# Cross attention and a gated feed-forward: the head's statements in another order

## The chip, the cores and the metric

The kernel runs on one core of a Trainium2 chip. The metric is device time in microseconds of one execution. TensorE is called PE, its weight loads PEld, VectorE DVE, ScalarE ACT, GpSimd POOL, SyncE SP. Only SP, ACT and POOL issue DMAs here.

## The reference

Two stages. `x` has the shape (B, H, S, D) = (8, 8, 512, 64), `state` (8, 8, 32, 64). The first stage lets tokens read the state and the state read the tokens; the second is a gated feed-forward over all 4352 = 8 x (512 + 32) rows of width 512.

```python
scores = scale * (x @ state.T)                # per batch and head: 512 x 32
a = softmax(scores)
xread = a @ state                             # 512 x 64
a2 = softmax(scale * (state @ x.T))           # 32 x 512
sread = a2 @ x                                # 32 x 64
h = concat([xread, sread], axis=2)            # rows of 512 after heads are joined
gate = sigmoid(h @ w_gate)                    # 512 -> 1536
out = (gate * (h @ w_val)) @ w_out            # 1536 -> 512
```

## The kernel before, in words

The order of all work is written out by hand: the program runs under a manual schedule, so each engine executes its instructions in the order of the statements, and waits on semaphores for what others make. PSUM is eight banks, `G0 G1 OU S0 S1 S2 S3 AT`; a statement that writes PSUM names its bank, and waits until the bank's last reader is done.

Work is staged by batch. For batch `b`: x is loaded and cast to bf16; `xT_mm`/`xT_cp` transpose it (PE, then an eviction; from batch 2 on `at_xT_dma` lets SP's DMA do it); `S_mm` (for batch 0 in quarters, `Sq_mm`) makes scores, `S_exp` (`Sq_exp`) the exponentials `E` on ACT; `n_sum`, `n_mul` (`nq_sum`, `nq_mul`) normalise to `ab`; `aT_mm`/`aT_cp` or `aT_dma` transpose that to `aT`. `at_Eb` casts `E` to bf16 on POOL (four instructions, L200), and `rd_mm`, `rd_fin` make what the state reads.

Tokens' feed-forward uses an identity: (a @ state) @ W = a @ (state @ W). `sw_visit(b, lo, n, bank, bank, *ws)` multiplies the state with columns `lo:lo+n` of the weights (L286, L293; without `ws` it takes gate and value at once), and `sw_cp` evicts to `SW`. `sw_wide` does three such visits. `gv_mm(b, f, bank, bank)` multiplies `aT` by 128 columns of `SW` for gate and value (four products of 512 columns), `gv_th` makes tanh on ACT (L364), `gv_glu` the gated product on DVE (L369).

The product with `w_out` is one level of a seven-product scheme (Strassen-like). It needs sums of quarter matrices: of `wo` (`ht_sum(t, eng)`, T0 to T3, L400, 128x1536) and of the gated values of batch 0 (`h_sum(t, half, eng)`, L407, 128x768). `h_mm(k, c)` does the products of batch 0 (L442): 1 and 2 need `wo` itself, 5, 6, 7 and 4 need T0 to T3.

The head, lines 563 to 837, does batches 0 and 1 to the end of their `gv_mm`, the output products of batch 0, and prepares batch 2. Then `step(b, f)` loops over batches 2 to 8 and twelve column blocks.

Loads in the head: x of batch 0 on SP's queue; x of batch 1 (`load_xh`, two halves), all weights (`load_w(w, lo, n)`, L104, w = 0 for gate and 1 for value), state pieces (`load_sb`, L527), x of batch 2 and `wo` (`load_wo`, L107) on POOL's queue. A DMA issue on POOL is an instruction in POOL's row, behind its casts, products and memsets:

```python
def load_w(w, lo, n):
    src = (moe_w_gate, moe_w_val)[w].rearrange("(k p) n -> p k n", p=128)
    nc.gpsimd.dma_start((wg, wv)[w][:, :, lo:lo + n], src[:, :, lo:lo + n])
```

`zero(sTz, pool)` clears the padded state matrix (128x2048), and `pad(2, 6)` fills it from `sTc`; `sT_mm(q)`, `sT_cp(q)` transpose state pieces. `warm(n, bank)` is n matmuls on zeros. `w_keep`, `w_add` and `h_U4` combine the seven products; `w_store` writes them out.

Of the kernel before, what the change touches and what calls it, by code (L numbers as in the profile page):

```python
# [16 lines left out]
def kernel(  # L17
# [14 lines left out]
    nc = tc.nc  # L32
# [93 lines left out]
    def xT_mm(b, j, place, n=1):  # L126

        ps = held["xT", b, j] = place[0].tile((128, n, 4, 128), BF, name="xTp", tag=place[1])
        for jj in range(n):
            for k in range(4):  # L130
                h, c = 2 * (j + jj) + k // 2, k % 2 * 2
                nc.tensor.transpose(ps[:, jj, k], xhs[b][:, h, c:c + 2].rearrange("p c d -> p (c d)"), ident)

    def xT_cp(b, j, cp, n=1):
        cp(xT_tile(b)[:, j:j + n], held["xT", b, j])
# [43 lines left out]
    def Sq_exp(b, j):  # L179
        if b not in E1s:  # L180
            E1s[b] = ap_.tile((128, 4, 2, 128), FP, name="E1")
        nc.scalar.activation(quarter(b, j, E1s), held["Sq", b, j].rearrange("p c e n -> p (c e) n"), AF.Exp, scale=scale)

    def nq_sum(b, j):
        rs = ap_.tile((128, 8), FP, name="rsq", bufs=4)
        nc.vector.tensor_reduce(rs, quarter(b, j, E1s), AX.X, ALU.add)
        ri = held["riq", b, j] = ap_.tile((128, 8), FP, name="riq", bufs=4)
        nc.vector.reciprocal(ri, rs)
# [411 lines left out]
    xT_mm(1, 0, S0, 2)  # L600
    nq_sum(0, 2)
    load_w(1, 1024, 256)
    xT_cp(0, 3, act)
    load_sb(2)
    Sq_mm(0, 3, OU)
    Sq_exp(0, 1)
    nq_sum(0, 0)
    nq_sum(0, 1)
    Sq_exp(0, 3)
    nq_sum(0, 3)  # L610
    load_w(1, 0, 256)
    warm(3, G0)
    nq_mul(0, 3, vec)
    xT_cp(1, 0, act, 2)
    nq_mul(0, 0, pool)
    xT_mm(1, 2, S1, 2)
    nq_mul(0, 2, vec)
    nq_mul(0, 1, pool)
    xT_cp(1, 2, vec, 2)
    S_mm(1, 0, OU)  # L620
    S_exp(1, 0)
    load_w(1, 1280, 256)
    n_sum(1, 0)
    at_Eb(0)
    aT_mm(0, AT)
    aT_cp(0, 0, act)
    S_mm(1, 1, S2)
# [3 lines left out]
    sw_cp(0, 256, 2, 0, vec)
    S_exp(1, 1)
    n_sum(1, 1)
    rd_mm(0, AT)
    sw_cp(0, 256, 2, 1, act)
    n_mul(1, 0, pool)
    rd_fin(0)
    load_w(0, 0, 256)
    load_sb(1)
    sw_visit(1, 256, 256, OU, S3)  # L640
    sw_cp(1, 256, 2, 0, act)
    load_sb(3)
    gv_mm(0, 3, G0, S1)
    n_mul(1, 1, vec)
    gv_th(0, 3)
    load_w(0, 512, 512)
    sw_visit(0, 1024, 256, G1, AT)
    sw_cp(1, 256, 2, 1, act)
    sw_visit(1, 1024, 256, OU, G0)
    sw_cp(0, 1024, 2, 1, act)  # L650
    load_w(1, 512, 512)
    sw_cp(0, 1024, 2, 0, act)
    at_Eb(1)
    sw_cp(1, 1024, 2, 0, act)
    aT_mm(1, S0)
    gv_glu(0, 3)
    aT_cp(1, None, vec)
# [96 lines left out]
    sw_cp(1, 1280, 2, 0, act)
    h_sum(2, 0, pool)
    h_sum(2, 1, vec)
    sw_cp(1, 1280, 2, 1, act)
    gv_mm(1, 4, G1, OU)
    gv_glu(1, 6)
    cast_x(2, pool, 0, 4)  # L760
    gv_mm(1, 7, S1, AT)
    gv_th(1, 4)
    sw_cp(1, 0, 2, 1, vec)
    gv_glu(1, 4)
    gv_th(1, 7)
    gv_glu(1, 7)
    gv_mm(1, 11, S3, G1)
    h_sum(1, 1, pool)
# [7 lines left out]
    h_sum(0, 0, pool)
    h_mm(5, 0, G1)
    S_mm(2, 0, OU)
    h_mm(5, 1)
    ht_sum(2, vec)  # L780
    h_sum(1, 0, vec)
# [254 lines left out]
```

## Time and profile before

| | us |
|---|---|
| median of 3 runs | 212.94 (212.85 to 213.03) |
| the profiled execution | 213.18 |
| its span, first to last instruction | 211.4 |
| PE busy | 203.4 |
| DVE busy | 160.5 |
| ACT busy | 129.8 |
| POOL busy | 78.6 |

The span is what the trace shows of the profiled execution; the 1.8 us beside it lie before the first and after the last instruction. Busy time is the union of an engine's instructions. A row of the timeline gives start, length, engine, line, operation, output <- inputs, count, and in brackets the idle time before it with what ended it. DMA rows give size and time from issue to landing.

### The profile page before, as it was taken

To read this page: it belongs to the slowest core of one execution; us is meant where nothing else is said; L and a number is where in the kernel's file an instruction comes from. 1 tells how busy PE (TensorE), PEld (TensorE's weight loads), DVE (VectorE), ACT (ScalarE), POOL (GpSimd) and SP (SyncE) were. 2 spreads that over 40 slices of the span, in tenths; PEclk is the share of its full clock that TensorE was granted. 3 is DMA by queue.
4 is the path that set the end of the run, shared out by engine and by line. 5 is a ranking of instruction groups with operands and counts; after the bars stand their busy time and mean duration, and the time that the engine had idled before them with its cause. 6 is when DMAs were issued, how large, how long until landed. Compare 5 with 4: busy or idle time off the path is not lost.

```text
span 211.4 us, 5331 instructions
## 1 busy us (share of the span) xinstructions
PE 203.4 (96%) x2089; PEld 132.1 (62%) x2089; DVE 160.5 (76%) x308; ACT 129.8 (61%) x244; POOL 78.6 (37%) x104
## 2 busy tenths in 40 slices
PE   7679999999999999999999999999999999999993
PEld 2445443677666656565656565656566666788982
DVE  2788889998987788578876887687848876864682
ACT  4978888754767477855786578647774673233210
POOL 8899358599042705900391029301500000000010
PEclk9999999999999999999999999999999999999999
DMA  6999999671689942995923611274110500130044
GB/s 205 180 192 191 227 277 179 113 214 38 80 220 349 123 93 85 301 104 141 312 65 48 195 78 28 58 110 164 29 31 0 202 2 0 74 128 0 3 172 125
DMA packets 40921, 27.14 MB, mean 128 GB/s; under 512 B 23617, under 2 KB 38721, under 8 KB 40897
## 3 DMA queue, kind: packets, MB, share of 16 engines
q1 hardware_dynamic: 30544, 19.47, 37.1%
q0 software_dynamic: 9920, 7.01, 20.4%
q10 hardware_dynamic: 432, 0.33, 0.6%
q8 instruction: 16, 0.26, 0.6%
q14 instruction: 9, 0.07, 0.2%
HBM read 18.35 MB, written 8.91 MB: 129 GB/s over the span
## 4 chain that ended last, share of the span: by engine, by line
PE 91%; DMA 4%; POOL 2%; issue 1%; DVE 0%; POOLq 0%
PE gvp L355 30%; PE outp L425 29%; PE gvp L343 10%; PE gvp L358 5%; PE outp L442 4%; DMA wgv<-in_moe_w_val_dram 4%; PE swp L286 4%; PE outp L484 2%; PE swp L293 2%; PE Sp L147 1%; PE outp L467 1%; POOL wgv L104 1%; PE rdp L262 1%; POOL xf L100 1%; PE rdp L265 0%
## 5 line engine op out<-in xcount | busy, mean ns | idle before, releaser
L369 DVE SCALAR_TENSOR_TENSOR glu<-th,gvp 128x512 bf16<-128x512 f32 (+1 forms) x108 | 70.1, 655 | 36.6 <-PE gvp L355 13.7
L364 ACT ACTIVATE th<-gvp 128x512 f32<-128x512 f32 (+1 forms) x108 | 62.1, 578 | 49.5 <-PE gvp L355 34.8
L355 PE MATMUL gvp<-aT,SW 128*128 128x512 bf16 x288 | 77.4, 379 | 0.1
L329 ACT CAST SW<-swp 128x512 bf16<-128x512 f32 x83 | 46.7, 593 | 9.3 <-PE swp L286 8.3
L425 PEld LDWEIGHTS <-Sm 128*128 128x128 bf16 x324 | 31.7, 98 | 12.6
L355 PEld LDWEIGHTS <-SW 128*128 128x128 bf16 x288 | 26.7, 98 | 17.3 <-issue 3.1
L200 POOL CAST Eb<-E 128x256 bf16<-128x256 f32 x32 | 12.8, 438 | 52.0 <-ACT E L167 52.0
L425 PE MATMUL outp<-tw,Sm 128*128 128x256 bf16 x240 | 31.8, 273 | 0.0
L425 PEld LDWEIGHTS <-glu 128*128 128x128 bf16 x240 | 23.5, 98 | 10.2
L425 PE MATMUL outp<-wo,glu 128*128 128x256 bf16 x168 | 22.9, 273 | 0.0
L343 PE MATMUL gvp<-aT,SW 128*128 128x512 bf16 x96 | 22.6, 379 | 0.0
L509 POOL DMA_DIRECT2D out_dram<-res x1 | 0.6, 613 | 50.3 <-DVE res L433 50.3
L227 POOL TENSOR_TENSOR ab<-E,ri 128x512 bf16<-128x512 f32 x13 | 14.3, 1100 | 11.8 <-DVE ri L210 7.1
L407 DVE TENSOR_TENSOR Sm<-glu 128x768 bf16<-128x768 bf16 (+1 forms) x34 | 18.0, 536 | 0.0
L433 DVE SCALAR_TENSOR_TENSOR res<-outp,U 128x512 f32<-128x512 f32 x22 | 15.1, 686 | 1.2 <-PE outp L442 0.9
L343 PEld LDWEIGHTS <-SW 128*128 128x128 bf16 x96 | 8.7, 98 | 10.5 <-issue 1.6
L116 POOL CAST xb<-xf 128x1024 bf16<-128x1024 f32 x12 | 13.2, 1126 | 2.3 <-DMA xf<-in_x_dram 2.3
L358 PE MATMUL gvp<-xb,wgv 128*128 128x256 bf16 x96 | 12.6, 273 | 0.0
L167 ACT ACTIVATE E<-Sp 128x512 f32<-128x512 f32 x14 | 8.4, 599 | 6.9 <-PE Sp L147 5.7
L425 PE MATMUL outp<-wo,Sm 128*128 128x256 bf16 x84 | 11.5, 273 | 0.0
L358 PEld LDWEIGHTS <-wgv 128*128 128x128 bf16 x96 | 9.3, 98 | 1.3
L251 POOL CAST xs<-xf 128x1024 bf16<-128x1024 f32 x10 | 10.1, 1039 | 0.0
(106 smaller groups left out, 221.6 us busy)
## 6 DMA issues: line engine op xcount, KB each, us to landing
out_dram<-res SPq DMA_DIRECT2D x14, 512.0 KB, 3.3
xf<-in_x_dram SPq DMA_DIRECT2D x5, 1024.0 KB, 7.5
wo<-in_moe_w_out_dram POOLq DMA_DIRECT2D x3, 512.0 KB, 8.1
xf<-in_x_dram SPq DMA_DIRECT2D x4, 256.0 KB, 3.7
wgv<-in_moe_w_gate_dram POOLq DMA_DIRECT2D x4, 256.0 KB, 7.3
wgv<-in_moe_w_val_dram POOLq DMA_DIRECT2D x4, 256.0 KB, 8.7
xf<-in_x_dram POOLq DMA_DIRECT2D x1, 1024.0 KB, 10.1
xf<-in_x_dram POOLq DMA_DIRECT2D x2, 256.0 KB, 5.9
```

The costliest lines, as they stand in the source:

```text
L116: cp(xbs[b].rearrange("p c h d -> p h c d")[:, lo:lo + n], (xhs if b in xhs else xfs)[b][:, lo:lo + n])
L200: nc.gpsimd.tensor_copy(Ebs[b][:, c], E1s[b][:, c])
L227: (nc.gpsimd if eng is pool else nc.vector).tensor_tensor(half(b, i, abs_), e1, ri.unsqueeze(len(ri.shape)).to_broadcast(e1.shape), ALU.mult)
L329: cp(*sw_left.pop((b, lo, w, e)))
L343: nc.tensor.matmul(ps, SWs[b][:, g, w, fs], aTs[b][:, :, g], start=(g == 0), stop=(g == 1))
L355: nc.tensor.matmul(ps, SWs[b][:, g, w, fs], aTs[b][:, :, g], start=(g == 0), stop=(g == 1))
L358: nc.tensor.matmul(ps, (wg, wv)[w][:, j, fs], held["XS"][:, j], start=(j == 0), stop=(j == 3))
L364: nc.scalar.activation(th, held["gv", b, f][0], AF.Tanh, scale=0.5)
L369: nc.vector.scalar_tensor_tensor(glus[b][:, f], held["th", b, f], 1.0, held["gv", b, f][1], ALU.add, ALU.mult)
L407: eng.tensor_tensor(S_(b, t)[:, i], a, c, op)
L425: nc.tensor.matmul(wps[key][:, c], lhs[:, i, c * 128:(c + 1) * 128], rhs[:, i], start=(first and c == 0 and i == 0), stop=(i == NF // 2 - ...
L433: nc.vector.scalar_tensor_tensor(to, wps[key], 0.5, held["w", name], ALU.mult, ALU.add)
```

## The change

Statements of the head from line 591 to line 837 stand in another order. The instructions are the same in kind and number, but for these: some evictions and sums run on another engine (among them `xT_cp(1, 0)` from ACT to DVE, `aT_cp(1)` from DVE to ACT, `sT_cp(3)` from ACT to DVE, `ht_sum(0)` and `ht_sum(2)` from DVE to POOL, `n_mul(2, 0)`, `h_sum(2, 0)`, `h_sum(0, 0)`, `h_sum(1, 1)`, `h_sum(3, 0)` from POOL to DVE, `h_sum(2, 1)` and `h_sum(3, 1)` from DVE to POOL), and most PSUM banks are others. Two lines of the diff stand for it:

```diff
-    sw_visit(0, 256, 256, G0, G1)
+    sw_visit(0, 256, 256, S3, OU)
...
-    ht_sum(0, vec)
+    ht_sum(0, pool)
```

POOL's queue between the first weight loads and the load of x for batch 2, before. `E_177` is the exponentials of batch 0, `E_265` those of batch 1; L104 rows are weight loads, L527 state pieces, L82 is x of batch 2:

```order
L527 DMA tw<-in_state_dram 128x4x64
L104 DMA wgv<-in_moe_w_val_dram 128x4x256
L193 TENSOR_TENSOR ab<-E_177,riq 128x8x32 x2
L104 DMA wgv<-in_moe_w_val_dram 128x4x256
L200 CAST Eb<-E_177 128x256 x4
L104 DMA wgv<-in_moe_w_gate_dram 128x4x256
L227 TENSOR_TENSOR ab<-E_265,ri 128x8x64
L104 DMA wgv<-in_moe_w_gate_dram 128x4x256
L527 DMA tw<-in_state_dram 128x4x64 x2
L104 DMA wgv<-in_moe_w_gate_dram 128x4x512
L104 DMA wgv<-in_moe_w_val_dram 128x4x512
L200 CAST Eb<-E_265 128x256 x4
```

The same stretch of POOL's queue after (`E_182` is batch 0, `E_320` batch 1, L111 is `zero(sTz)`):

```order
L527 DMA tw<-in_state_dram 128x4x64
L193 TENSOR_TENSOR ab<-E_182,riq 128x8x32 x2
L200 CAST Eb<-E_182 128x256 x4
L193 TENSOR_TENSOR ab<-E_182,riq 128x8x32
L200 CAST Eb<-E_320 128x256 x4
L104 DMA wgv<-in_moe_w_val_dram 128x4x256
L227 TENSOR_TENSOR ab<-E_320,ri 128x8x64
L111 MEMSET sTz 128x2048
L104 DMA wgv<-in_moe_w_val_dram 128x4x256
L654 MEMSET xs 128x32x2
L104 DMA wgv<-in_moe_w_gate_dram 128x4x256 x2
L527 DMA tw<-in_state_dram 128x4x64 x2
```

The two value-weight loads (`load_w(1, 0, 256)` and `load_w(1, 1280, 256)`) moved behind both batches' casts, and the second of them behind `n_mul(1, 0)` and `zero(sTz)` as well; the rest of the loads follow in the same order as before, x of batch 2 and all three of `wo` directly behind the last weights.

POOL's queue toward the end of the head, before (from the load of the last third of `wo` to `n_mul` of batch 2, L227):

```order
L107 DMA wo<-in_moe_w_out_dram 128x4x512
L407 TENSOR_TENSOR Sm<-glu 128x768
L116 CAST xb<-xf 128x4x4x64
L407 TENSOR_TENSOR Sm<-Sm,glu 128x768
L407 TENSOR_TENSOR Sm<-glu 128x768
L407 TENSOR_TENSOR Sm<-glu,Sm 128x768
L227 TENSOR_TENSOR ab<-E_911,ri 128x512 x2
```

And after, from the three loads of `wo` on:

```order
L107 DMA wo<-in_moe_w_out_dram 128x4x512 x3
L116 CAST xb<-xf 128x4x4x64 x2
L407 TENSOR_TENSOR Sm<-glu 128x768
L557 COPY sTz<-sTc 64x24x32 x2
L400 TENSOR_TENSOR tw<-wo 128x1536 x2
L407 TENSOR_TENSOR Sm<-glu,Sm 128x768
L227 TENSOR_TENSOR ab<-E_852,ri 128x512
```

Two of POOL's four sums of gated values left it, two sums of `wo` (L400, twice as long in elements) came, and one of the two `n_mul` of batch 2 went to DVE.

On PE `rd_mm(0)` and `rd_mm(1)` stand earlier (`rd_mm(1)` before the first `gv_mm`, where it stood behind twelve of them), `sT_mm(3)` later, `warm(3)` some 2 us of work earlier. The products of batch 0 begin with `h_mm(2, 0)`, after twenty `gv_mm` instead of twenty-two.

More of the change, by code (lines that the diff above doesn't have):

```diff
@@ L601 @@
     nq_sum(0, 2)
[L602 to L605, printed above, removed]
+    xT_cp(1, 0, vec, 2)
+    Sq_mm(0, 3, G1)
     Sq_exp(0, 1)
-    nq_sum(0, 0)
+    xT_mm(1, 2, G0, 2)
+    nq_mul(0, 0, pool)
     nq_sum(0, 1)
+    xT_cp(1, 2, vec, 2)
     Sq_exp(0, 3)
+    S_mm(1, 0, S0)
     nq_sum(0, 3)
-    load_w(1, 0, 256)
[L612 to L618, printed above, removed]
@@ L619 @@
-    xT_cp(1, 2, vec, 2)
-    S_mm(1, 0, OU)
-    S_exp(1, 0)
-    load_w(1, 1280, 256)
[L623 to L627, printed above, removed]
-    load_w(0, 1280, 256)
-    aT_cp(0, 1, act)
-    sw_visit(0, 256, 256, G0, G1)
[L631 to L637, printed above, removed]
+    nq_mul(0, 2, pool)
+    S_mm(1, 1, OU)
+    at_Eb(0)
+    nq_mul(0, 1, vec)
+    rd_mm(0, S2)
@@ new lines @@
+    nq_mul(0, 3, pool)
+    nc.scalar.activation(pre[:, 0:1], ones, AF.Exp)
+    S_exp(1, 0)
+    aT_mm(0, AT)
+    S_exp(1, 1)
+    at_Eb(1)
+    rd_fin(0)
+    n_sum(1, 0)
+    load_w(1, 0, 256)
+    sw_visit(0, 256, 256, S3, OU)
+    aT_cp(0, 0, act)
+    n_mul(1, 0, pool)
+    sw_visit(1, 256, 256, G1, S1)
+    zero(sTz, pool)
+    aT_cp(0, 1, act)
+    sw_cp(0, 256, 2, 1, act)
+    rd_mm(1, S0)
+    sw_cp(0, 256, 2, 0, vec)
+    n_sum(1, 1)
+    gv_mm(0, 2, S3, S2)
+    sw_cp(1, 256, 2, 1, act)
@@ new lines @@
+    n_mul(1, 1, vec)
+    gv_th(0, 2)
+    load_w(1, 1280, 256)
+    sw_cp(1, 256, 2, 0, act)
+    sw_visit(1, 1024, 256, AT, OU)
+    rd_fin(1)
+    sw_visit(0, 1024, 256, G0, S1)
+    sT_mm(2, S3)
+    aT_mm(1, G1)
+    sw_cp(0, 1024, 2, 0, vec)
+    sT_cp(2, vec)
+    nc.gpsimd.memset(xs[:, :, :, D:], 1.0)
+    sw_cp(1, 1024, 2, 1, act)
+    sw_cp(0, 1024, 2, 1, act)
+    sw_cp(1, 1024, 2, 0, vec)
+    gv_mm(0, 3, S0, OU)
+    aT_cp(1, None, act)
+    load_w(0, 1280, 256)
+    gv_mm(0, 9, G0, S1)
@@ L642 @@
+    sT_mm(1, AT)
+    sw_cp(0, 0, 2, 1, act)
     load_sb(3)
-    gv_mm(0, 3, G0, S1)
-    n_mul(1, 1, vec)
-    gv_th(0, 3)
+    gv_glu(1, 3)
+    sw_cp(0, 0, 2, 0, vec)
+    gv_mm(1, 9, OU, G1)
     load_w(0, 512, 512)
[L647 to L650, printed above, removed]
-    load_w(1, 512, 512)
[L652 to L657, printed above, removed]
@@ L764 @@
-    gv_glu(1, 4)
[L765 to L768, printed above, removed]
+    sT_cp(1, act)
+    gv_mm(0, 1, G0, S2)
+    gv_th(1, 9)
+    gv_glu(0, 8)
+    gv_mm(0, 0, S3, S0)
+    load_w(1, 512, 512)
+    gv_glu(1, 9)
+    gv_th(0, 1)
+    sw_visit(0, 512, 512, G1, OU, 0)
+    gv_th(0, 0)
+    gv_glu(0, 1)
+    sw_cp(0, 512, 0, 1, vec)
+    sw_cp(0, 512, 0, 0, act)
+    gv_glu(0, 0)
+    gv_mm(0, 10, S1, AT)
+    gv_mm(0, 11, G0, S3)
+    gv_th(0, 10)
+    gv_th(0, 11)
@@ new lines @@
+    sT_cp(3, vec)
+    gv_glu(1, 5)
+    gv_mm(1, 6, G1, OU)
+    gv_th(1, 6)
+    sw_visit(1, 1280, 256, AT, G0)
+    h_sum(0, 0, vec)
+    h_sum(2, 1, pool)
+    sw_cp(1, 0, 2, 1, act)
+    sw_cp(1, 1280, 2, 1, act)
+    h_sum(2, 0, vec)
+    at_xT_dma(2)
+    sw_cp(1, 1280, 2, 0, act)
+    gv_mm(1, 7, S3, S1)
+    gv_mm(1, 4, G1, G0)
+    h_sum(1, 0, vec)
+    pad(2, 6)
+    S_mm(2, 0, S2)
+    h_sum(3, 0, vec)
+    ht_sum(0, pool)
+    gv_th(1, 7)
+    h_mm(2, 0, AT)
+    gv_th(1, 4)
+    gv_glu(1, 6)
@@ new lines @@
+    sw_cp(1, 0, 2, 0, act)
+    S_exp(2, 0)
+    ht_sum(2, pool)
+    h_mm(2, 1)
+    gv_glu(1, 7)
+    h_mm(1, 0, S3)
+    S_mm(2, 1, S0)
+    h_mm(1, 1)
+    gv_glu(1, 4)
+    n_sum(2, 0)
+    h_sum(1, 1, vec)
+    gv_mm(1, 10, G0, S1)
+    ht_sum(1, vec)
+    h_mm(5, 0, G1)
+    h_sum(3, 1, pool)
+    gv_th(1, 10)
+    w_keep('V1', 1)
+    S_exp(2, 1)
+    h_mm(5, 1)
+    gv_mm(1, 1, G0, OU)
+    load_x(3, nc.sync)
+    n_mul(2, 0, vec)
+    h_mm(6, 0)
+    h_mm(6, 1)
+    w_add(2, 'V1', w_res(0, 0)[:, :, lo_])
@@ L769 @@
+    gv_th(1, 1)
+    gv_glu(1, 1)
+    w_keep('U2', 1)
+    gv_mm(1, 0, AT, S2)
+    n_sum(2, 1)
+    n_mul(2, 1, pool)
+    gv_th(1, 0)
+    gv_glu(1, 10)
+    gv_mm(1, 11, G0, S3)
+    aT_dma(2, 0)
     gv_th(1, 11)
-    at_xT_dma(2)
-    gv_mm(1, 10, G0, S1)
+    gv_glu(1, 0)
+    cast_x(3, pool, 4, 4)
     gv_glu(1, 11)
-    h_mm(1, 0, AT)
-    h_mm(1, 1)
-    ht_sum(0, vec)
[L776 to L781, printed above, removed]
```

234 lines of the change are left out of this document (82 added, 152 removed).

## Prediction

> **What bounds the kernel now.** I read the page's span and busy times first, then the busy time by stretches, to see where TensorE (PE) is idle at all.
>
> ```profile
> span 211.4 us, 5331 instructions
> PE 203.4 (96%) x2089; PEld 132.1 (62%) x2089; DVE 160.5 (76%) x308; ACT 129.8 (61%) x244; POOL 78.6 (37%) x104
> ```
>
> ```profile
> 0.00:16.00 16.00, 11.83 (x167) 6.13 (x167) 9.78 (x28) 11.12 (x20) 14.80 (x27) 1.00 1.16 192
> 16.00:53.00 37.00, 36.98 (x442) 20.64 (x434) 33.29 (x56) 26.97 (x53) 27.59 (x31) 1.00 0.94 176
> ```
>
> Columns: stretch, length, then busy time of PE, PEld, DVE, ACT and POOL, granted clock, DMA share, GB/s. PE idles 4.2 us before 16 us and 0.02 us from there to the end of the head at 53. So the most that any order of the head can win is a part of 4.2 us, and whatever makes PE wait after 16 us is paid in full, for no gap is left to absorb it. POOL is the engine to look at beside it, with 14.80 of the first 16 us busy. DMA moves 192 GB/s there, so each 256 KB block takes 1.3 us of the stream.
>
> The stream is fed by POOL. Its rows, in order of time, show where the weight loads (L104) stand among its other work:
>
> ```profile
> 8.01 0.77 POOL L104 DMA_DIRECT2D wgv<-in_moe_w_val_dram  x1
> 9.35 1.19 POOL L193 TENSOR_TENSOR ab<-E,riq 128x256 bf16<-128x256 f32 x2 [0.57 <-DVE riq L188]
> 10.48 0.81 POOL L104 DMA_DIRECT2D wgv<-in_moe_w_val_dram  x1
> 11.28 1.42 POOL L200 CAST Eb<-E 128x256 bf16<-128x256 f32 x4
> ...
> 17.40 0.79 POOL L104 DMA_DIRECT2D wgv<-in_moe_w_val_dram  x1
> 18.13 1.47 POOL L200 CAST Eb<-E 128x256 bf16<-128x256 f32 x4
> 19.50 1.84 POOL L111 MEMSET sTz<- 128x2048 bf16 x1
> 21.25 0.93 POOL L82 DMA_DIRECT2D xf<-in_x_dram  x1
> ```
>
> The DMA view gives issue to landing. Its rows below are those of the first x load on POOL's queue (issued at 2.73), `load_w(1, 0, 256)` (8.01), `load_w(1, 1280, 256)` (10.48), `load_w(1, 512, 512)` (17.40), `load_wo(2)` (32.34), and, for comparison, four x loads on SP's queue:
>
> ```profile
> xf<-in_x_dram POOLq DMA_DIRECT2D x1, 256.0 KB, 5.3
> wgv<-in_moe_w_val_dram POOLq DMA_DIRECT2D x1, 256.0 KB, 9.3
> wgv<-in_moe_w_val_dram POOLq DMA_DIRECT2D x1, 256.0 KB, 8.4
> wgv<-in_moe_w_val_dram POOLq DMA_DIRECT2D x1, 512.0 KB, 11.0
> wo<-in_moe_w_out_dram POOLq DMA_DIRECT2D x1, 512.0 KB, 6.4
> xf<-in_x_dram SPq DMA_DIRECT2D x4, 256.0 KB, 3.7
> ```
>
> Issue plus landing time: the five POOL loads land at 8.0, 17.3, 18.9, 28.4 and 38.7 us. A wait of 8 to 11 us for 256 or 512 KB, where the same bytes need 1.3 or 2.6 us, is queueing: POOL issues far ahead, and the stream is never empty. What PE waits for at the end of that stream stands in its weight-load rows:
>
> ```profile
> 28.46 0.14 PEld L286 LDWEIGHTS <-tw 64*32 64x32 bf16 x16 [0.31 <-DMA wgv<-in_moe_w_val_dram]
> ```
>
> At 28.46 PE starts the first product with `wgv[512:1024]` of the value weights, 0.05 us after they landed. This gate has no slack: delay the stream by d and PE is late by d.
>
> **The change part by part.** *Loads on POOL.* In the new order `load_w(1, 0, 256)` stands behind `at_Eb(1)`, and `load_w(1, 1280, 256)` behind `n_mul(1, 0, pool)` and `zero(sTz, pool)`. When is `at_Eb(1)` free to run? It casts the exponentials of batch 1, and these hang on the second half of its x:
>
> ```profile
> 10.19 0.62 PE L132 MATMUL xTp<-ident,xf 128*128 128x128 bf16 x8 [0.43 <-DMA xf<-in_x_dram]
> 10.64 0.40 PE L156 MATMUL Sp<-tw,xT 128*128 128x64 bf16 x8
> 11.08 0.60 ACT L167 ACTIVATE E<-Sp 128x512 f32<-128x512 f32 x1 [0.64 <-PE Sp L156]
> 11.27 0.68 DVE L135 COPY xT<-xTp 128x1024 bf16<-128x1024 bf16 x1
> ```
>
> Transposes from 10.19 (unchanged: they wait for a DMA), eviction, scores, exponential: 10.2 + 0.62 + 0.68 + 0.40 + 0.60, some 12.6 with the hand-offs. POOL has `nq_mul(0, 3, pool)` ahead (0.6, half of the 1.19 row), whose sum DVE makes only after that eviction, at 11.5; it ends at about the same time, so 12.7 is a fair start. Then 1.4 for the four casts: `load_w(1, 0, 256)` is issued at 14.1, not 8.0. Its issue takes 0.77, `n_mul` 1.10 (POOL's row for L227, below) and `zero` 1.84: `load_w(1, 1280, 256)` at 17.8, not 10.5, when the load before it, landing near 18.7, is all that the stream still holds. So it starts on a nearly empty stream. How long it then takes no row shows. The nearest are 5.3 (the first load, beside SP's four), 5.1 (6.4 for 512 KB, less 1.3 for the second half, at a time when the stream had run low) and, from below, SP's 3.7. I take 4.6, between them, since nothing runs beside it; the ends are 3.7 and 5.3. It lands at 22.4 instead of 18.9: the stream is 3.5 us late (2.6 to 4.2).
>
> Behind it everything is issued in time (POOL has no other work until all of it is out, some 26 us), in the order of before, so landings keep their distance: `load_w(1, 512, 512)` 28.4 - 18.9 = 9.5 behind, at 31.9; `load_wo(2)` 19.8 behind, at 42.2.
>
> The Trainium skill ("DMA: Bandwidth & Descriptors", section "Anatomy of one DMA — SWDGE (gpsimd) path") gives about 2.0 us fixed plus bytes at 436 GB/s; by that page 256 KB would land in an estimated 2.6 us and the sum below would be some 2 us smaller. The 5.3 and 5.1 of this trace speak against it.
>
> *PE at the gate.* Until the gate PE does the same twelve `gv_mm` as before. `rd_mm(1)` moves ahead of it, `sT_mm(3)` and one `sw_visit` behind it. Costs from the chain of waits:
>
> ```profile
> 28.46 0.63 PE swp L286 x16
> 29.09 0.35 PE rdp L265 x32
> 29.43 0.28 PE rdp L268 x8
> ...
> 44.12 0.23 PE Sp L147 x8
> 44.35 0.86 PE gvp L343 x4
> 45.22 0.66 PE outp L442 x6
> ```
>
> A `gv_mm` is 0.86, a visit 0.3, `rd_mm` 0.63, `S_mm` (and `sT_mm`, also eight small products) 0.23, an `h_mm` 0.66. Net work behind the gate: 0.63 - 0.3 - 0.23, 0.1 less. PE is late by 31.9 - 28.46 - 0.1 = **3.3 us**. What PE saves before 16 us (`rd_mm(0)` and `rd_mm(1)` now fill the wait for the first weights) is worth nothing, since it waits longer at the gate; the same cover pays for the moved `warm(3)` and for `xT_cp(1, 0)` on DVE and `aT_cp(1)` on ACT. If the stream were not late, the gate at 28.4 would still hold, and the saving would be that 0.1.
>
> *wo and the first h_mm.* After the gate stand 3 visits, 8 `gv_mm`, `sw_wide` (as 3 visits), 2 visits, `sT_mm` and `S_mm`: 0.9 + 6.9 + 0.9 + 0.6 + 0.5 = 9.8 (a visit's own row counts 0.1 of drain, which I take off once), so `h_mm(2, 0)` comes at 41.6. Its last two products need `load_wo(2)`, 0.44 later at 42.0 against 42.2: **0.2**. In the old order ten `gv_mm` stood here.
>
> *T sums on POOL.* `ht_sum(0)` and `ht_sum(2)` go from DVE to POOL, twice the length of POOL's other sums:
>
> ```profile
> L400 DVE TENSOR_TENSOR tw<-wo x2: 951/952/954, 40.0 to 40.8; 128x1536 bf16<-128x1536 bf16 x2
> L407 POOL TENSOR_TENSOR Sm<-glu 128x768 bf16<-128x768 bf16 x2 | 3.3, 1640 | 0.3 <-DVE glu L369 0.3
> L407 POOL TENSOR_TENSOR Sm<-glu,Sm 128x768 bf16<-128x768 bf16 x1 | 2.3, 2291 | 2.4 <-DVE Sm L407 2.4
> L227 POOL TENSOR_TENSOR ab<-E,ri 128x512 bf16<-128x512 f32 x13 | 14.3, 1100 | 11.8 <-DVE ri L210 7.1 <-DVE rr L273 4.5
> L116 POOL CAST xb<-xf 128x1024 bf16<-128x1024 f32 x12 | 13.2, 1126 | 2.3 <-DMA xf<-in_x_dram 2.3
> ```
>
> Twice 1.64 to 2.29 is 3.3 to 4.6 where DVE took 0.95. Started at 42.2 when wo is there, T0 is ready at 45.5 to 46.8. `h_mm(5, 0)` needs it, after the rest of `h_mm(2, 0)` (0.22), three `h_mm`, `S_mm` and a `gv_mm`: 42.2 + 3.3 = 45.5. A wait of 0 to 1.3; I take **0.4**, nearer the 1.64 that two of three such sums took. The Trainium skill ("GPSIMD Engine Reference", section "4.1 Engine selection") calls POOL about twice as slow as DVE for such sums; by that estimate T0 takes 1.9 and this term is nothing. The rows here say more than three times.
>
> *What else hangs on POOL and SP.* Batch 2 goes through both twice: x lands, POOL casts it, SP transposes it for `S_mm`; later POOL finishes `ab`, SP transposes that for the steady loop. SP's transposes, and the first product of the loop:
>
> ```profile
> xf<-in_x_dram POOLq DMA_DIRECT2D x1, 1024.0 KB, 10.1
> xT<-xb SPq DMA_TRANSPOSE x24, 2.5
> 35.99 5.21 SPq L140 DMA_TRANSPOSE xT<-xb  x4
> 53.57 0.61 PE L355 MATMUL gvp<-aT,SW 128*128 128x512 bf16 x2
> ```
>
> x was issued at 21.25, landed at 31.35, and now lands 3.5 later at 34.9. Two casts of 1.13, then transposes issued 1.3 apart, each landing in 2.5: the second, which `S_mm(2, 0)` needs, at 41.0 (PE comes at 41.4), the fourth, for `S_mm(2, 1)`, at 43.6 (PE: 43.7). Just hidden, 0 to 0.5. Then T2 (3.3), `h_sum(3, 1)` (1.64), `n_mul(2, 1)` (1.10) and two transposes (1.3 + 2.5) follow T0: 45.5 + 9.8 = 55.3, up to 4 us more with the slower sums, against 53.57 + 3.9 = 57.5 for the loop's first product. Hidden, 0 to 1.5. `n_mul(2, 0)` on DVE leaves POOL 1.1 for less than that there. Other evictions and sums change engine, but DVE (33.29 of 37 us) and ACT (26.97) keep gaps: 0, up to 0.3 if a bank is late.
>
> *Sum.* 3.3 + 0.2 + 0.4 = 3.9 us. The profiled execution took 213.18 (span 211.4), 0.24 above the median of 212.94; it would become 217.1, the median **216.8**.
>
> **The rivals.**
>
> *The empty stream answers fast.* If a load on an empty queue lands like the smallest store,
>
> ```profile
> out_dram<-res SPq DMA_DIRECT2D x1, 64.0 KB, 1.8
> ```
>
> plus 1.3 for its bytes, in 3.1, then `load_w(1, 1280, 256)` lands at 20.9, the gate opens at 30.4 (PE 1.8 late), and with 0.2 + 0.4 the time is 215.3. For it: nothing runs beside the load. Against it: 5.3 and 5.1 on this very queue. The skill's page named above, with its 2.6, would end near 214.8.
>
> *POOL's tail decides.* All its sums at 2.29 a half: T0 costs 1.3 and the steady loop waits 0.9 for `aT`: 3.3 + 0.2 + 1.3 + 0.9 = 5.7, 218.6. For it: the 2.29 row, taken while DVE summed too, as it will again. Against: two of three rows at 1.64.
>
> *Late, but not felt.* The weights are late by less than PE's new lead. The lead is 0.1, and a time within 0.2% (0.43 us, about what a measurement of this kernel can tell from no change) leaves room for 0.5 in all. But issued at 17.8 and with 1.3 us of bytes the load can't land before 19.1, 0.2 later than before, so this takes a load that starts at once, or a POOL that is through by 14. It would end at 213.0.
>
> *Faster: the stream catches up.* After its pauses every queue is drained, and the 9.5 us from `load_w(1, 1280, 256)` to the gate could shrink. Below 28.4 - 22.4 = 6.0 us the gate opens earlier than before, and PE, with `rd_mm` done early, gains: at 5.2, 0.8 us, 212.1. Against it: those 9.5 us hold two blocks of 256 KB, two of 64 and two of 512, 1.66 MB, which at the stream's 192 GB/s take 8.7.
>
> **How the numbers follow.** Forecast 0.60, fast empty stream 0.17, POOL's tail 0.15, not felt 0.05, faster 0.03. So slower 0.92, same 0.05, faster 0.03. The range runs from 214.8, a little under the fast stream's case, to 218.8, just over the POOL tail's; it covers 3.7 to 5.3 for the landing (215.9 to 217.5 with the rest as summed).
>
> **What would show it.** In the changed kernel: L104 issues near 14.1 and 17.8; a dip in GB/s near 15 and 19; landing times of 4 to 5 us for `load_w(1, 1280, 256)`; PE idle of some 4 us between 21 and 32, released by DMA of `wgv`, longest before `sw_visit(0, 1280, 256)` and the 512-wide visits; 3.3 us or more a T sum on POOL. Wrong would be: PE idle 0 there, POOL getting to `load_w(1, 0, 256)` before 11 us, or a granted clock under 1.00 in the new gaps.

## The result and the profile after

The changed kernel takes 222.7 us (median of 4 runs, 221.95 to 223.07), the kernel before beside it 212.99 (212.85 to 213.55): a ratio of 1.044 [1.040, 1.047], 9.7 us slower. The forecast was 3.9 us slower, its range ended at 218.8. The profiled execution took 223.06 us.

Span, PE's busy row and the same kind of stretches as before, now of the changed kernel (its head ends near 63):

```profile
span 221.3 us, 5326 instructions
PE 207.1 (94%) x2089; PEld 133.3 (60%) x2089; DVE 166.7 (75%) x309; ACT 129.3 (58%) x243; POOL 81.6 (37%) x104
```

```profile
0.00:16.00 16.00, 12.54 (x183) 7.12 (x184) 8.49 (x25) 8.83 (x18) 13.22 (x27) 0.93 1.04 177
16.00:63.00 47.00, 39.79 (x412) 21.02 (x419) 40.56 (x59) 28.90 (x55) 31.65 (x31) 0.99 0.88 148
```

PE idles 3.5 us before 16 us (4.2 before the change) and 7.2 us behind it, where it had idled 0.02. Its busy time grew as well, by 3.7 us, in part because the clock was low near 14 to 17 us. What it waits for, in the table of waits (us in total, times, longest):

```profile
PE Sp L147 <- DMA xT<-xb: 2.7, 2, 2.5
PE swp L293 <- DMA wgv<-in_moe_w_gate_dram: 2.0, 1, 2.0
PE gvp L343 <- DVE res L433: 1.2, 1, 1.2
...
PE outp L442 <- DVE tw L400: 0.6, 1, 0.6
...
PE swp L286 <- DMA wgv<-in_moe_w_val_dram: 0.4, 1, 0.4
PE outp L442 <- DVE res L433: 0.4, 1, 0.4
```

The forecast spoke of the two `wgv` lines. The scores of batch 2 waiting for transposed x (`xT`), and the three lines released by DVE, it had at 0 to 0.8 us together; they are 4.9.

First the part that was foreseen. POOL's timeline gives the issues of the two value-weight loads, and the DMA view their time to landing and that of `load_w(1, 512, 512)`:

```profile
14.74 0.81 POOL L104 DMA_DIRECT2D wgv<-in_moe_w_val_dram  x1
15.57 1.06 POOL L227 TENSOR_TENSOR ab<-E,ri 128x512 bf16<-128x512 f32 x1
16.56 1.81 POOL L111 MEMSET sTz<- 128x2048 bf16 x1
18.31 0.81 POOL L104 DMA_DIRECT2D wgv<-in_moe_w_val_dram  x1
...
22.85 0.78 POOL L104 DMA_DIRECT2D wgv<-in_moe_w_val_dram  x1
```

```profile
wgv<-in_moe_w_val_dram POOLq DMA_DIRECT2D x1, 256.0 KB, 4.0
wgv<-in_moe_w_val_dram POOLq DMA_DIRECT2D x1, 512.0 KB, 9.6
```

18.31 + 4.0 puts `load_w(1, 1280, 256)` at 22.3, 3.4 later than before; 22.85 + 9.6 puts the last value weights at 32.45. PE's timeline shows the gate and the places behind it:

```profile
25.19 0.41 PE L293 MATMUL swp<-wgv,tw 64*32 64x512 bf16 x8 [1.95 <-DMA wgv<-in_moe_w_gate_dram]
...
32.48 0.84 PE L286 MATMUL swp<-wgv,tw 64*32 64x512 bf16 x24 [0.39 <-DMA wgv<-in_moe_w_val_dram]
...
44.93 0.29 PE L147 MATMUL Sp<-sTz,xT 128*128 128x64 bf16 x4 [2.52 <-DMA xT<-xb]
...
52.22 1.48 PE L442 MATMUL outp<-tw,Sm 128*128 128x256 bf16 x12 [0.62 <-DVE tw L400]
54.86 1.46 PE L343 MATMUL gvp<-aT,SW 128*128 128x512 bf16 x6 [1.16 <-DVE res L433]
...
63.71 1.04 PE L355 MATMUL gvp<-aT,SW 128*128 128x512 bf16 x4
```

The gate opens at 32.48 instead of 28.46, and the steady loop's first product comes at 63.71 instead of 53.57. So of 10.1 us, 4.0 arise up to the gate and 6.1 behind it, and these 6.1 the forecast had at 0.6.

Where they arise is seen on DVE and POOL side by side, DVE first:

```profile
48.31 3.85 DVE L400 TENSOR_TENSOR tw<-wo,tw 128x1536 bf16<-128x1536 bf16 x1
52.09 2.12 DVE L227 TENSOR_TENSOR ab<-E,ri 128x512 bf16<-128x512 f32 x1
54.13 0.68 DVE L433 SCALAR_TENSOR_TENSOR res<-outp,V 128x512 f32<-128x512 f32 x1
```

```profile
44.88 6.47 POOL L400 TENSOR_TENSOR tw<-wo 128x1536 bf16<-128x1536 bf16 x2 [2.48 <-DMA wo<-in_moe_w_out_dram]
51.31 2.35 POOL L407 TENSOR_TENSOR Sm<-glu,Sm 128x768 bf16<-128x768 bf16 x1
```

DVE's T1 took 3.85 us where such a sum took 0.95 before. It starts while POOL does T2 (the second of POOL's two T sums) and ends at 52.16, 0.8 after POOL's end at 51.35, about its own length. `n_mul(2, 0)` starts beside POOL's `h_sum(3, 1)` and ends 0.55 after that one's end. The `w_add` behind them (L433) at 54.13 frees the bank for which `gv_mm(1, 0)` waits.

The readings to test: **A**, the late weight loads; **B**, the transposes of batch 2 go slowly because the `w_out` loads still stream beside them; **C**, a two-input sum on DVE stands still while POOL does one. The rival to all is the granted clock, which fell to 0.50 near 14 to 17 us.

### The profile page after: what moved, and what is told of

The parts are those of the page before. It is cut to its first block, busy times and chain, and to the rows that moved or that the text cites. A ratio compares the mean times of both kernels' runs of the same rounds, so it can differ in the third digit from the quotient of the medians.

```text
span 221.3 us, 5326 instructions
## 1 busy us (share of the span) xinstructions
PE 207.1 (94%) x2089; PEld 133.3 (60%) x2089; DVE 166.7 (75%) x309; ACT 129.3 (58%) x243; POOL 81.6 (37%) x104
## 4 chain that ended last, share of the span: by engine, by line
PE 71%; DMA 11%; POOL 6%; DVE 6%; issue 3%; SPq 1%; ACT 0%; DVEq 0%; POOLq 0%; ACTq 0%
PE gvp L355 29%; PE outp L425 28%; DMA xf<-in_x_dram 9%; PE gvp L358 5%; DMA xT<-xb 3%; PE swp L286 3%; PE outp L484 2%; POOL wgv L104 2%; DVE tw L400 2%; PE outp L467 1%; PE Sp L147 1%; DVE glu L369 1%; PE swp L293 1%; DVE ab L227 1%; POOL xb L116 1%
## 5 line engine op out<-in xcount | busy, mean ns | idle before, releaser
L200 POOL CAST Eb<-E 128x256 bf16<-128x256 f32 x32 | 13.5, 454 | 51.7 <-ACT E L167 51.7
L407 DVE TENSOR_TENSOR Sm<-glu 128x768 bf16<-128x768 bf16 (+1 forms) x35 | 20.0, 576 | 0.0
L227 POOL TENSOR_TENSOR ab<-E,ri 128x512 bf16<-128x512 f32 x12 | 12.6, 1050 | 14.2 <-DVE ri L210 9.5
L433 DVE SCALAR_TENSOR_TENSOR res<-outp,U 128x512 f32<-128x512 f32 x22 | 15.0, 683 | 0.7 <-PE outp L442 0.4
L329 DVE CAST SW<-swp 128x512 bf16<-128x512 f32 x13 | 8.8, 686 | 4.4 <-PE swp L293 3.3
L407 DVE TENSOR_TENSOR Sm<-Sm,glu 128x768 bf16<-128x768 bf16 (+1 forms) x18 | 10.0, 555 | 0.2
```

The lines of the kernel that those rows point to most:

```text
L200: nc.gpsimd.tensor_copy(Ebs[b][:, c], E1s[b][:, c])
L227: (nc.gpsimd if eng is pool else nc.vector).tensor_tensor(half(b, i, abs_), e1, ri.unsqueeze(len(ri.shape)).to_broadcast(e1.shape), ALU.mult)
L329: cp(*sw_left.pop((b, lo, w, e)))
L407: eng.tensor_tensor(S_(b, t)[:, i], a, c, op)
L433: nc.vector.scalar_tensor_tensor(to, wps[key], 0.5, held["w", name], ALU.mult, ALU.add)
```

## The experiments

### The loads alone, in the order of before

The kernel before, with POOL's order of casts, loads and fills from the change: `load_w(1, 0, 256)` behind `at_Eb(1)`, the later loads behind `n_mul(1, 0)` and `zero`.

```diff
     n_sum(1, 1)
+    at_Eb(1)
+    load_w(1, 0, 256)
+    n_mul(1, 0, pool)
+    zero(sTz, pool)
+    load_w(1, 1280, 256)
+    load_w(0, 1280, 256)
...
```

> The kernel before, with one thing of the change alone: the order of the weight loads on POOL's queue (at_Eb(1) ahead of load_w(1,0,256), then n_mul(1,0) and zero, then the other loads). Theory A (the late weight stream costs PE 4.0 us at the gate before the product sums, and nothing else of the change belongs to it): load_w(1,0,256) is issued near 14.5 us instead of 8.0, the w_val tile of 512 columns lands about 32 instead of 28.4, and the kernel takes 216.0 to 217.2 us. If the loads also push the x2 and w_out loads behind them into the transposes of batch 2, 218.5 to 219.5. Rival (the loads are late but not felt; the loss comes from the sums and the transposes): 212.8 to 213.5.

Measured: 219.4 us (218.45 to 221.26), ratio 1.028 [1.026, 1.031]. That is more than theory A's 216.0 to 217.2. The number lies in the expectation's second range, but by luck: PE waits for no transposes here. In this order the first late tile that PE needs is `load_w(0, 0, 256)`, which lands behind `load_w(0, 1280, 256)`, the first that the changed kernel needs; so the pause is longer, and the clock falls behind it. PE's timeline, and the clock by stretches (the third column from the right):

```profile
27.60 1.06 PE L293 MATMUL swp<-wgv,tw 64*32 64x512 bf16 x16 [4.24 <-DMA wgv<-in_moe_w_gate_dram]
28.59 3.59 PE L343 MATMUL gvp<-aT,SW 128*128 128x512 bf16 x8
```

```profile
27.00:33.00 6.00, 5.40 (x41) 2.41 (x42) 2.69 (x5) 2.62 (x5) 0.00 (x0) 0.50 1.26 231
```

Eight products take 3.59 us; the same eight take 1.90 at full clock, in the next run. The four runs of this kernel had mean clocks of 0.981 (221.26 us), 0.980 (219.59), 0.992 (219.21) and 0.999 (218.45). So even the run with hardly any loss of clock is 5.5 us above the kernel before: that is the lateness.

### The same, with PE kept busy in the pause

```diff
+    warm(18, AT)
     sw_visit(0, 0, 256, AT, S2)
```

> The kernel before with the late weight loads (219.4 us), and 18 matmuls without use on PE in the 4.2 us in which it waits for the first late tile. If the half-speed clock of 26.7 to 33.7 us (7 us at 0.50, some 3 us of work lost) comes from that pause of PE, the granted clock stays at 1.00 and the time falls to 216 to 217.3 us, with the wait for the tile itself unchanged. If the clock falls for another reason, or its loss is hidden by the gate, the time stays at 218.5 to 220.

Measured: 218.65 us (218.12 to 219.32), ratio 1.026 [1.022, 1.029]. The clock by stretches, in the same place:

```profile
27.00:33.00 6.00, 5.94 (x62) 2.69 (x60) 4.68 (x8) 4.64 (x10) 1.27 (x2) 1.00 1.20 238
```

With PE busy in the pause there is no half-speed stretch in the profiled execution, so the pause is its likely cause. But it seems that a pause doesn't always bring it: one of the four runs above, without the extra matmuls, had a mean clock of 0.999 (its trace is not at hand). The median fell by only 0.75 us, not 2 to 3, and the two sets of runs overlap: what is left is the lateness itself. The profiled execution of this kernel starts the steady loop at 58.51, 4.9 after 53.57. I had carried 4.0 us over from the changed kernel, and this order has 4.9 of it.

### The changed kernel with early loads

```diff
...
     load_sb(2)
+    load_w(1, 0, 256)
+    load_w(1, 1280, 256)
...
     n_sum(1, 0)
+    load_w(0, 1280, 256)
+    load_w(0, 0, 256)
+    n_mul(1, 0, pool)
+    load_w(0, 512, 512)
...
```

> The changed kernel, with the weight loads of value row 1 issued early again, right behind load_sb(2), and the other weight loads behind n_sum(1,0). Theory A: the gate comes back to within 0.7 us of 28.5, 4 us are won there; if the transposes of batch 2 and the slowed sums cost what they cost in the changed kernel, 218 to 219 us. If the early stream also takes the w_out loads away from the transposes, 215.5 to 216.5. Rival (the loads are not the cause): 222 to 223.

Measured: 222.87 us (222.29 to 223.5), ratio 1.046 [1.044, 1.049]: nothing won, as the rival had it. But the gate did come earlier, at 30.10, and the wait for `xT` fell to 0.74. The time went elsewhere: PE, DVE and POOL of this run, in that order:

```profile
48.97 1.87 PE L343 MATMUL gvp<-aT,SW 128*128 128x512 bf16 x4 [4.73 <-DVE glu L369]
```

```profile
40.33 3.44 DVE L407 TENSOR_TENSOR Sm<-Sm,glu 128x768 bf16<-128x768 bf16 x1
43.80 3.32 DVE L407 TENSOR_TENSOR Sm<-glu,Sm 128x768 bf16<-128x768 bf16 x1
47.05 1.87 DVE L369 SCALAR_TENSOR_TENSOR glu<-th,gvp 128x512 bf16<-128x512 f32 x3
```

```profile
40.08 6.63 POOL L400 TENSOR_TENSOR tw<-wo 128x1536 bf16<-128x1536 bf16 x2
```

With `wo` there earlier, POOL starts its two T sums at 40.08, and now they meet two `h_sum` of DVE, each 3.3 to 3.4 us: each lasts about as long as one T sum. Such a sum in the kernel before:

```profile
41.72 0.55 DVE L407 TENSOR_TENSOR Sm<-Sm,glu 128x768 bf16<-128x768 bf16 x1
```

The `gv_glu` behind the two start at 47.05, and PE stands still for 4.73 us, followed by 0.50 clock near 49 to 52. Late weights had kept these sums apart.

### The changed kernel with its two T sums on DVE

```diff
-    ht_sum(0, pool)
...
-    ht_sum(2, pool)
...
+    ht_sum(0, vec)
     n_sum(2, 0)
...
     ht_sum(1, vec)
+    ht_sum(2, vec)
```

> The changed kernel, with the two T sums that it gave to POOL (ht_sum(0) and ht_sum(2)) back on DVE. Theory C (VectorE and GpSimd slow each other while both run sums of two inputs): ht_sum(1) takes 1.0 us on DVE instead of 3.85, the waits ahead of h_mm(6,0), gv_mm(1,0) and h_mm(4,0), 2.1 us together, are gone, and the kernel takes 220.3 to 221.0 us. Rival (those waits end with other work that is just as late, the clock or the transposes): 222.2 to 222.8.

Measured: 220.18 us (219.63 to 222.47), ratio 1.036 [1.030, 1.041]. Theory C's 220.3 to 221.0, a little better. `ht_sum(1)` is back at its length, and the T sum that meets POOL's remaining `h_sum(3, 1)` (50.14 to 52.35) is stretched instead. Its DVE rows:

```profile
49.91 0.95 DVE L400 TENSOR_TENSOR tw<-wo,tw 128x1536 bf16<-128x1536 bf16 x1
50.77 2.39 DVE L400 TENSOR_TENSOR tw<-wo 128x1536 bf16<-128x1536 bf16 x1
```

### Both together

The early loads (here with the two state loads ahead of the 512-column ones) and the T sums on DVE.

```diff
...
     n_sum(1, 0)
+    load_w(0, 1280, 256)
+    load_w(0, 0, 256)
+    load_sb(1)
+    load_sb(3)
+    n_mul(1, 0, pool)
...
+    ht_sum(0, vec)
...
+    ht_sum(2, vec)
...
```

> The changed kernel with both edits: the weight loads early (the two state loads now ahead of the 512-column tiles) and the two T sums of POOL on DVE. Apart they moved the time by +0.2 and -2.5 us. If each edit hides the other's loss (with early loads the first two T sums on POOL start near 40 us, beside DVE's sums of the products, and hold those up), the two together win much more than their sum: the wait of 4.7 us ahead of gv_mm(1,10) and the half-speed clock behind it go, and the kernel takes 214.8 to 216.5 us. If the effects simply add: 220.2 to 220.6. The product-sum gate is expected near 29.5 us (30.1 with the early loads alone, 32.5 in the changed kernel).

Measured: 218.31 us (217.75 to 219.68), ratio 1.025 [1.020, 1.030]. The prices don't add (medians, us):

| | T sums on POOL | T sums on DVE |
|---|---|---|
| loads late | 222.7 | 220.2 |
| loads early | 222.9 | 218.3 |

Early loads win 1.9 us once POOL no longer holds DVE up, and nothing while it does. That the time stayed above the expected 214.8 to 216.5 has two places, seen in its waits, which the next runs take up:

```profile
PE gvp L343 <- DVE res L433: 2.0, 1, 2.0
PE aTp L234 <- POOL ab L227: 1.4, 1, 1.4
```

### No w_out loads beside the transposes

The changed kernel without its second and third `w_out` load (1.0 MB), which sets two thirds of `w_out` to zero on DVE at the start.

```diff
+    nc.vector.memset(wo[:, 4:12], 0.0)
...
-    load_wo(1)
-    load_wo(2)
```

> The changed kernel without its second and third w_out load: two thirds of w_out are set to zero, so the last product leaves out two thirds of its weights. It takes 1.3 MB or so out of the stream between the x2 load and the transposes of batch 2. Theory B (the transposes are slow because the w_out loads still stream beside them): the transposes land 2.5 to 3.5 us after issue instead of 7.4, the wait of 2.5 us ahead of the scores of batch 2 is gone, and the kernel takes 219.7 to 220.5 us. Rival (the transposes are slow for a reason of their own): 222.2 to 222.9 with the wait in its place.

Measured: 225.2 us (224.4 to 225.5), ratio 1.057 [1.054, 1.059]: slower, where B expected a gain. On its own point B is right. The transposes in the DMA view, first of the changed kernel, then of this run:

```profile
xT<-xb SPq DMA_TRANSPOSE x4, 5.7
```

```profile
xT<-xb SPq DMA_TRANSPOSE x4, 2.5
```

The wait ahead of the scores of batch 2 fell from 2.52 to 0.05 us. But POOL's T sums started earlier (43.51), met DVE's `h_sum`, and PE's only long wait behind 40 us is

```profile
PE gvp L343 <- DVE glu L369: 5.7, 1, 5.7
```

the same place as with early loads. Part of the extra time lies at the start, where PE waited 2.5 us for x of batch 1 (0.7 in the changed kernel) and the clock was 0.51 from 14 to 21 us; the gate opens at 33.53, 1.0 later. Why that load was late isn't shown.

### One more POOL instruction, that reads or that only writes

The kernel before, with work on POOL that nobody needs, in a region of `tw` that is free then.

```diff
     h_sum(0, 0, pool)
+    pr = tw[:, -1024:]
+    nc.gpsimd.tensor_tensor(pr, pr, pr, ALU.subtract)
```

> The kernel before with one more instruction on POOL, that nobody needs: a two-input subtraction of 1024 bf16 columns (some 2.2 us) behind h_sum(0,0), at 40.0 us, while DVE does its T sums. Theory C, that a two-input sum on DVE and a POOL instruction that reads SBUF exclude each other for the whole instruction: one of DVE's T sums, 0.95 us alone, takes 2.5 to 3.2 us, the product that needs it (h_mm(5,0) at 41.1 or h_mm(7,0) at 42.6) is late by about as much less its slack, and the kernel takes 214.2 to 215.3 us. If the two engines only slow each other by their share of a port: DVE's sums 1.0 to 1.9 us, 213.2 to 214.0. If there is nothing between them: 212.9 to 213.1.

Measured: 214.56 us (214.34 to 214.72), ratio 1.0068 [1.0048, 1.0088]: +1.6 us, theory C. POOL, DVE and PE rows:

```profile
39.71 1.89 POOL L778 TENSOR_TENSOR tw<-tw 128x1024 bf16<-128x1024 bf16 x1
```

```profile
39.76 3.52 DVE L400 TENSOR_TENSOR tw<-wo 128x1536 bf16<-128x1536 bf16 x2
```

```profile
42.46 0.82 PE L442 MATMUL outp<-tw,Sm 128*128 128x256 bf16 x6 [1.42 <-DVE tw L400]
```

POOL took 1.89 us, not the 2.2 expected. DVE starts 0.05 us behind it; its two T sums take 3.52 us and end at 43.28. POOL's end (41.60) plus the 1.82 that the two take alone would be 43.42. So it is not a shared rate: the first sum gets next to nothing until POOL is done. The control has two fills in that place.

```diff
     h_sum(0, 0, pool)
+    pr = tw[:, -1024:]
+    nc.gpsimd.memset(pr, 0.0)
+    nc.gpsimd.memset(pr, 0.0)
```

> The control of the run with the extra POOL subtraction: at the same place two POOL fills of the same 1024 columns (some 1.9 us together), which write SBUF and read nothing. The Trainium skill, page "SBUF — State Buffer", section "Who interferes with whom", says that a DVE instruction with two SBUF inputs contends with a GpSimd instruction that reads SBUF, and not with one that only writes it. By an exclusion of readers alone the kernel takes 212.9 to 213.2 us and DVE's T sums keep 0.95 us. If any POOL instruction holds DVE's sums up: 214.0 to 215.0, with T sums of 2 to 3 us.

Measured: 212.95 us (212.87 to 213.42), ratio 0.9992 [0.9977, 1.0008]: no change. Again POOL, then DVE:

```profile
39.62 0.95 POOL L778 MEMSET tw<- 128x1024 bf16 x1
40.62 0.95 POOL L779 MEMSET tw<- 128x1024 bf16 x1
```

```profile
39.69 1.82 DVE L400 TENSOR_TENSOR tw<-wo 128x1536 bf16<-128x1536 bf16 x2
```

The same 1.9 us of POOL beside the same two sums, and they take 1.82. The two runs agree with what the control's expectation takes from the Trainium skill ("SBUF — State Buffer", section "Who interferes with whom").

### The T sums alone, in the kernel before

```diff
-    ht_sum(0, vec)
+    ht_sum(0, pool)
...
-    ht_sum(2, vec)
+    ht_sum(2, pool)
```

> The kernel before with one part of the change alone: its first and third T sum (ht_sum(0), ht_sum(2)) on POOL in place of DVE, at the same place in the order. POOL does them at 38.4 to 41.6 us and, behind h_sum(0,0), at 43.2 to 46.4. By the prediction's price (POOL's time, and DVE untouched) h_mm(5,0) waits 0.4 us and the kernel takes 213.0 to 213.8 us. By the exclusion of DVE's two-input sums while POOL reads SBUF, h_sum(1,0) and ht_sum(1) on DVE end only after POOL's sums, ht_sum(1) near 47 instead of 43.1, h_mm(6,0) at 43.3 waits for it, and the kernel takes 215.5 to 218 us.

Measured: 218.06 us (216.99 to 219.1), ratio 1.023 [1.017, 1.029]. The number is about the upper end of what was expected of the exclusion (215.5 to 218), but by luck: the way there is another. POOL, then PE:

```profile
39.76 3.09 POOL L400 TENSOR_TENSOR tw<-wo 128x1536 bf16<-128x1536 bf16 x1 [1.64 <-PE gvp L343]
42.81 1.63 POOL L407 TENSOR_TENSOR Sm<-glu 128x768 bf16<-128x768 bf16 x1
44.40 3.08 POOL L400 TENSOR_TENSOR tw<-wo 128x1536 bf16<-128x1536 bf16 x1
```

```profile
44.49 1.46 PE L442 MATMUL outp<-tw,Sm 128*128 128x256 bf16 x6 [3.46 <-POOL Sm L407]
```

`h_mm(5, 0)` also needs `h_sum(0, 0)`, and that stands behind T0 in POOL's queue: ready at 44.44. So the long sum first costs by its place in the queue (3.46 us), and then by the clock, which is 0.50 from 45 to 50 us in the profiled execution. DVE's stretched `h_sum(1, 0)` (3.42 us) lies behind that. The run at clock 1.000 still took 216.99 us.

### What is left

`n_mul(1, 0)` ahead of the six later loads in the run with both edits:

```diff
     n_sum(1, 0)
+    n_mul(1, 0, pool)
     load_w(0, 1280, 256)
...
-    n_mul(1, 0, pool)
```

> The run with early loads and the T sums on DVE (218.3 us), with n_mul(1,0) on POOL ahead of the six later weight loads in place of behind four of them: there PE waited 1.4 us for it ahead of aT_mm(1). If that wait is passed on to the end, 216.8 to 217.3 us; if PE stalls for other things by as much, 218.0 to 218.5.

Measured: 217.29 us (216.85 to 218.28), ratio 1.020 [1.016, 1.024]. PE's wait of 1.4 us for `n_mul` is gone, and the gate opens at 28.98, 0.5 after that of before. The longest wait that is left behind the gate, 1.6 us for DVE, is the same collision once more: DVE's T2 starts at 45.15 beside POOL's `h_sum(3, 1)` (44.52 to 46.73) and takes 2.40 us.

And with every product sum on the engine of before:

```diff
...
-    h_sum(2, 1, pool)
+    h_sum(2, 1, vec)
...
-    n_mul(2, 0, vec)
+    n_mul(2, 0, pool)
...
```

> The run with the loads behind n_mul(1,0), with the engine of every product sum as in the kernel before as well (four h_sums and n_mul(2,0) to POOL, two h_sums to DVE); the order of the statements and the PSUM banks stay those of the changed kernel. If the rest of the loss lies in DVE's load of sums (gv_mm(1,0) waits 2.0 us for a bank that DVE frees late), the kernel takes 214.3 to 215.3 us, and order and banks alone cost about 2 us. If they cost nothing, 212.8 to 213.5. If POOL's sums hold DVE's up again, 217 to 219.

Measured: 216.22 us (215.83 to 217.58), ratio 1.017 [1.011, 1.022]: above the 214.3 to 215.3 expected, though the wait for DVE ahead of `gv_mm(1, 0)` is gone. Order and banks, with the evictions that stayed on their new engines, keep some 3.2 us. Some 1.2 us of it are more small waits (4.1 us in its table of waits against 2.9 before, without the 1.0 at the start; 0.8 of them for `xT`); the rest stays open.

From PE's timelines, the gate, the loop's first product, and what lies between (one profiled execution each):

| kernel | gate | loop | between |
|---|---|---|---|
| before | 28.46 | 53.57 | 25.1 |
| changed | 32.48 | 63.71 | 31.2 |
| changed, loads early | 30.10 | 62.93 | 32.8 |
| changed, T sums on DVE | 34.61 | 63.30 | 28.7 |
| both, `n_mul` ahead | 28.98 | 57.69 | 28.7 |
| and sums as before | 29.16 | 56.16 | 27.0 |

With early loads, from the third row down, the T sums cost 4.1 us (with the half clock behind the wait of 4.73), the engines of the other sums 1.7, order and banks 1.9. For the changed kernel itself such differences are no clean prices: in the fourth row the clock fell ahead of the gate in the profiled execution, the gate came later, and PE waited 1.0 us for `xT` instead of 2.7. There the waits are the better account of the 6.1 us: 2.7 for `xT`, 2.2 for DVE's late sums and evictions, and 1.2 that has no wait of its own (PE is busy 26.37 us between gate and loop, where it was 25.11); what that is stays open. None of these versions beats the kernel before.

## Why the prediction was wrong

The sign was right, and the mechanism that it forecast is there; but it makes 4.0 of the 10.1 us up to the steady loop. The other 6.1 lie in terms that it had at nearly nothing: 0.2 for `wo`, 0 to 0.5 for the transposes, 0.4 for the T sums, 0 to 0.3 for the other sums on DVE.

*Loads on POOL: right.* Issues forecast at 14.1 and 17.8, measured 14.74 and 18.31. Landing forecast 4.6 us after issue, measured 4.0. The estimate of 2.6 that the prediction worked out from the Trainium skill ("DMA: Bandwidth & Descriptors", section "Anatomy of one DMA — SWDGE (gpsimd) path") and set aside was too low here. The stream was 3.4 us late, forecast 3.5; that this is so close is luck, for an issue 0.5 later and a landing 0.6 faster cancel.

*PE at the gate: right, 4.0 for 3.3.* The landings did not quite keep their distance: 10.1 us from `load_w(1, 1280, 256)` to the last value weights, not 9.5. That the clock would fall was named as a sign of error. It fell to 0.50 near 14 to 17 us, but ahead of a gate set by DMA, where it costs little: the run of the changed kernel at clock 1.000 took 221.95 us, the others 222.35 to 223.07. At full clock it is still 9.0 us slower than before, so the clock is not the cause of the loss.

*wo and the first h_mm, 0.2, and the transposes, "Just hidden, 0 to 0.5": wrong by 2.5 us.* `load_wo(2)` was forecast to land at 42.2. Its rows have 26.73 for the issue and 17.8 to landing, 44.5; the transposes start at 37.44. First these, then the first transpose before the change:

```profile
26.73 0.74 POOL L107 DMA_DIRECT2D wo<-in_moe_w_out_dram  x1 [0.65 <-DMA wgv<-in_moe_w_gate_dram]
37.44 6.29 SPq L140 DMA_TRANSPOSE xT<-xb  x4
wo<-in_moe_w_out_dram POOLq DMA_DIRECT2D x1, 512.0 KB, 17.8
xT<-xb SPq DMA_TRANSPOSE x2, 7.0
```

```profile
xT<-xb SPq DMA_TRANSPOSE x1, 3.5
```

The first step that failed is this one: it priced the transposes at 2.5 us, the median of all 24, and didn't see that `wo` would now still stream when they start. Before, `wo` had landed at 38.7, and even so the first transpose, issued at 35.99, took 3.5 us. In the changed kernel the pair needed for `S_mm(2, 0)` landed 7.0 us after issue, and without two `wo` loads the four took 2.5. Faster transposes alone would not have won all of the wait: PE was ready for `S_mm(2, 0)` at 42.41, so by the prediction's own count `h_mm(2, 0)` would have needed the last `wo` at 43.1 and waited some 1.4 us for it (an estimate from these rows).

*T sums on POOL, 0.4: the right duration and the wrong victim.* This is the second step that failed. T0 and T2 took 6.47 us together, just under the forecast 3.3 each. `h_mm(5, 0)` didn't wait for them; PE had already been held. The price was paid on DVE, by "Other evictions and sums change engine, but DVE (33.29 of 37 us) and ACT (26.97) keep gaps: 0, up to 0.3 if a bank is late" and by "`n_mul(2, 0)` on DVE leaves POOL 1.1 for less than that there". `n_mul` took 2.12 us on DVE, and PE waited 2.2 us for DVE's late sums and evictions. That step looked for room in DVE's busy time and took each sum's length as its own; what decides is which POOL instruction runs at that moment. Undoing the two T sums won 2.5 us with late loads and 4.6 with early ones (there with the state loads moved too).

The sign of it stood in the prediction's own rows. Of the three `h_sum` on POOL that it shows, one took 2.29 us against 1.64 (a fourth, which it doesn't count, took 1.89). I called that "while DVE summed too" and let it lengthen POOL's sums in a rival; that DVE can be the one to stand, for as long as the POOL sum lasts, I did not ask. The Trainium skill ("SBUF — State Buffer", section "Who interferes with whom") says so: a DVE instruction with two SBUF inputs and a GpSimd instruction that reads SBUF share a port, the one that comes first has it to its end, and the other waits wholly. The added POOL reader and the added POOL fills agree with it on both sides.

*The rivals.* "POOL's tail decides" (218.6) was nearest, with a longer chain behind T0, though its mechanism, a late `aT`, isn't the one that was seen. The fast empty stream, with its 3.1 to landing, is refuted by the 4.0; "not felt" and "the stream catches up" by the gate at 32.48.

## What to carry to other kernels

Before a sum moves between VectorE and GpSimd, lay the two engines' timelines side by side. Count a DVE sum with two inputs from SBUF as ending only after the POOL instruction that it meets, if that one reads SBUF. And a lateness can keep two things apart: here it hid a collision that made PE wait 4.7 us, so price edits together, or run them as a two-by-two table.

## What the runs showed of the hardware

- A two-input sum on DVE that starts while POOL does an instruction that reads SBUF ends about its own length after POOL's end: 0.55 us became 3.3 to 3.4 beside a T sum, 0.95 became 3.85. A cast on POOL, with one input, does it too: T3 on DVE took 1.71 in the changed kernel and ended 0.8 after POOL's casts (60.25 against 59.44). POOL waits likewise when DVE is first (in the kernel before, 1.64 became 2.29 at 42.35, with T1 on DVE from 42.18). Beside POOL fills, DVE's sums kept their 0.95. DVE's reduction (0.69 at 46.44 in the changed kernel, during POOL's T sums) kept its length.
- The five pauses of PE of 3.5 to 5.7 us in these traces are each followed by half clock: 0.50 for about 7 us after 4.2 us of waiting with the late loads alone, about 3 us after 4.7 us with the early ones. With 18 idle matmuls in the pause it was 1.00. Shorter pauses go either way: 2.5 us of waiting for `xT` in the changed kernel brought no fall, 2.0 us with both edits did, and near 14 us in the changed kernel the clock fell behind waits of 0.7 us and less. The Trainium skill ("TensorE: Matmul & The Clock Gate", section "What's actually happening") gives an activity window of some 3.4 us, which fits these lengths as one or two windows.
- Transposes on SP's queue landed 7.0 us after issue (the first two) while 512 KB loads of POOL's queue were still streaming, and 2.5 with two of these loads removed.
